# First K tiles ahead of the second group's transposes, R's first mixes two slots later, dummy matmuls between stages

## The chip, the cores and the metric

One Trainium2 chip, one core. The metric is device time in microseconds (us) of one execution. Several executions of the kernel before and of the other kernel are timed in turn on the same chip. Each set of runs is compared only with the runs of before that were taken beside it.

A ratio is the mean time of one kernel's fast runs over that of the other's of the same rounds, so not quite the ratio of the medians that are quoted. "Over before" in us is the difference of those two means.

## The reference

A causal depthwise convolution of seven taps with softmaxed weights per head, then an RWKV channel mix on its result:

```python
w = softmax(weight)                                   # 8 heads x 7 taps
y[b, t, h, :] = sum_k w[h, k] * x[b, t + k - 6, h, :]  # zeros ahead of t = 0
xk = mu_k * y + (1 - mu_k) * y_prev                    # y_prev: y one step earlier
xr = mu_r * y + (1 - mu_r) * y_prev
k = relu(xk @ w_k)            # 192 -> 1024
v = (k * k) @ w_v             # 1024 -> 192
out = sigmoid(xr @ w_r) * v   # x: 8 x 4160 x 192, float32
```

## The kernel before

Work goes in groups of 120-token blocks. For a group, PE convolves by Toeplitz matrices, ScalarE copies the result to `y`, and PE transposes it (early groups) into PSUM, from where VectorE (DVE) copies it to `yT`. From `yT` DVE takes the difference of neighbouring tokens and mixes it into `xk` and `xr`. Then, for each "slot", PE computes a K tile, ScalarE applies relu, DVE squares. R and V products follow some slots later. The program sets the order of each engine's instructions.

Everything that the change touches is in the prologue and in the first few slots:

```python
    psK = ctx.enter_context(tc.tile_pool(name="psK", bufs=2, ...))   # K tiles, dummies
    psM = ctx.enter_context(tc.tile_pool(name="psM", bufs=2, ...))   # conv, transposes, R
    four = ctx.enter_context(tc.tile_pool(name="four", bufs=4))      # relu results
    # ...
        warm = psK.tile([P, BANK], FP32, tag="k", name="warm")
        for _ in range(WARM):                       # WARM = 40
            nc.tensor.matmul(out=warm, lhsT=ones_t, rhs=zeros, start=True, stop=True)
        # ... softmax, Toeplitz matrix, loads of x, K weights, R weights, V weights
        for t in tails:
            nc.gpsimd.memset(t, 0.0)
        # ... convolution of group 0 and its copies
        for j in range(2):
            tr_mm(0, j)
        for j in range(2):
            tr_out(0, j, dve_)
        n = len(chunks(1))
        for c in range(n):
            conv_mm(1, c, ...)
            conv_out(1, c, act_)
        diff(0)
        for i in range(2):                          # i = 0: xk, i = 1: xr
            for part in range(2):
                mix(0, i, part)
        for j in range(2):                          # second group: transposes and copies
            tr_mm(1, j)
            tr_out(1, j, dve_)
        # ...
    # per pair of slots: K tiles, then by slot: act table, pe table, relu, dve table,
    # and the square of the slot before
```

## Time and profile before

| | before |
|---|---|
| timed ahead of the prediction, median of 3 | 467.15 us (466.83 to 467.34) |
| timed beside the changed kernel, median of 6 | 466.99 us (464.91 to 467.39) |
| the execution that the profile shows | 466.09 us, span 464.4 us |
| granted clock of PE over the span | 0.993, half from 14.5 to 21.4 us |

The difference between the time and the span is what lies outside the first and last instruction. Times in timelines count from the start of the span.

### The profile page before, as it was taken

The numbers are of one execution on the slowest core, as the hardware profiler recorded it, in microseconds if no ns is written. First come the engines' busy times: TensorE is split into PE (matmuls) and PEld (weight loads), VectorE is DVE, ScalarE is ACT, GpSimd is POOL, SyncE is SP. The second block draws the span as 40 slices with busy tenths as digits, with TensorE's granted clock in tenths as the row PEclk, the third lists the DMA queues.
The fourth block names the chain that finished last, engine by engine and source line by source line (L and its number), as shares of the span: only waits on it lengthen the run. The fifth ranks groups of instructions, "written<-read, shape, count | busy, mean of one in ns | idle before, by whom it ended". The sixth has DMA issues, their size and how long they took to land.

```text
span 464.4 us, 10001 instructions
## 1 busy us (share of the span) xinstructions
PE 445.4 (96%) x3898; PEld 298.3 (64%) x3960; DVE 387.3 (83%) x748; ACT 371.3 (80%) x544; POOL 49.5 (11%) x71
## 2 busy tenths in 40 slices
PE   8787999999999999999999999999999999999996
PEld 3554666666876666566676666666677666666676
DVE  2887799887998889889798989878898987888873
ACT  2598878978878897888979788887978888777771
POOL 6810511000020050000002041000002000000000
PEclk9799999999999999999999999999999999999999
DMA  5993999683469599755367779938166753821223
GB/s 79 164 185 75 181 196 202 120 192 112 105 136 186 141 154 232 148 145 135 99 150 124 182 120 215 220 82 200 55 150 129 165 133 95 167 69 52 69 69 95
DMA packets 134480, 64.18 MB, mean 138 GB/s; under 512 B 85825, under 2 KB 133985, under 8 KB 134433
## 3 DMA queue, kind: packets, MB, share of 16 engines
q1 hardware_dynamic: 96097, 48.60, 41.9%
q0 software_dynamic: 38336, 14.95, 27.7%
q8 instruction: 31, 0.51, 0.5%
q14 instruction: 16, 0.13, 0.1%
HBM read 29.65 MB, written 37.25 MB: 144 GB/s over the span
## 4 chain that ended last, share of the span: by engine, by line
PE 91%; DMA 2%; DVE 2%; ACT 2%; issue 2%; POOL 0%; DVEq 0%
PE ps_k L346 39%; PE ps_v L436 37%; PE ps_r L418 5%; PE ps_r L419 5%; PE ps_c L199 4%; DMA xb<-in_x_dram 1%; ACT k_sb L375 1%; PE ps_k L363 1%; DMA w_raw<-in_weight_dram 1%; ACT y L219 1%; PE ps_t L257 1%; DMA w_scr<-w_row 1%; DVE k L394 0%; ACT y L222 0%; DVE yT L268 0%
## 5 line engine op out<-in xcount | busy, mean ns | idle before, releaser
L375 ACT ACTIVATE k_sb<-ps_k 128x1024 bf16<-128x1024 f32 x260 | 260.1, 1026 | 36.4 <-PE ps_k L346 31.6
L346 PE MATMUL ps_k<-xk,wk 64*128 64x512 bf16 (+2 forms) x994 | 205.3, 377 | 7.5 <-ACT k_sb L375 0.4
L436 PE MATMUL ps_v<-wv,k 128*128 128x192 bf16 x2048 | 210.8, 246 | 0.0
L436 PEld LDWEIGHTS <-k 128*128 128x128 bf16 x2048 | 175.3, 98 | 31.3 <-issue 1.8
L394 DVE TENSOR_TENSOR k<-k_sb 128x1024 bf16<-128x1024 bf16 x256 | 174.9, 685 | 15.0 <-ACT k_sb L375 14.3
L346 PEld LDWEIGHTS <-wk 64*128 64x128 bf16 (+1 forms) x1056 | 56.3, 96 | 109.1 <-issue 108.0
L449 DVE TENSOR_TENSOR o_sb<-ps_v,r_sb 128x384 f32<-128x384 f32 x132 | 72.4, 549 | 35.7 <-PE ps_v L436 33.8
L426 ACT ACTIVATE r_sb<-ps_r 128x384 bf16<-128x384 f32 x132 | 64.4, 488 | 39.3 <-PE ps_r L419 38.8
L418 PE MATMUL ps_r<-wr,xr 128*128 128x192 bf16 x256 | 62.9, 246 | 0.0
L419 PE MATMUL ps_r<-wr,xr 128*128 128x192 bf16 x256 | 62.9, 246 | 0.0
L219 ACT CAST y<-ps_c 120x384 bf16<-120x384 f32 (+4 forms) x96 | 45.0, 471 | 8.8 <-PE ps_c L199 8.8
L199 PE MATMUL ps_c<-xb,toe 128*128 128x384 bf16 (+6 forms) x152 | 43.5, 321 | 4.1 <-ACT y L222 1.8
L323 DVE TENSOR_TENSOR xr<-xr,yT 128x1024 bf16<-128x1024 bf16 (+1 forms) x66 | 36.2, 549 | 2.3
L323 DVE TENSOR_TENSOR xk<-xk,yT 128x1024 bf16<-128x1024 bf16 (+1 forms) x66 | 36.2, 549 | 2.3
L109 POOL DMA_DIRECT2D xb<-in_x_dram x38 | 33.5, 888 | 31.0 <-issue 17.5
L281 DVE TENSOR_TENSOR d<-yT 128x1536 bf16<-128x1536 bf16 (+2 forms) x37 | 31.8, 859 | 3.6 <-DMA yT<-y_dram 3.5
L320 DVE TENSOR_SCALAR xr<-d,mu 128x1024 bf16<-128x1024 bf16 (+1 forms) x66 | 27.9, 423 | 0.1
L108 POOL DMA_DIRECT2D xb<-in_x_dram x8 | 4.4, 552 | 221.1 <-PE ps_k L346 221.1
L320 DVE TENSOR_SCALAR xk<-d,mu 128x1024 bf16<-128x1024 bf16 (+1 forms) x66 | 26.6, 403 | 0.2
L418 PEld LDWEIGHTS <-xr 128*128 128x128 bf16 x256 | 25.0, 98 | 0.0
L419 PEld LDWEIGHTS <-xr 128*128 128x128 bf16 x256 | 25.0, 98 | 0.0
L222 ACT CAST y<-ps_c 120x384 bf16<-120x384 f32 (+9 forms) x52 | 24.0, 466 | 0.4 <-DVE yT L227 0.2
(48 smaller groups left out, 88.5 us busy)
## 6 DMA issues: line engine op xcount, KB each, us to landing
out_dram<-o_sb SPq DMA_DIRECT2D x128, 192.0 KB, 2.4
xb<-in_x_dram POOLq DMA_DIRECT2D x18, 384.0 KB, 10.4
y_dram<-y SPq DMA_DIRECT2D x6, 720.0 KB, 5.4
y_dram<-y SPq DMA_DIRECT2D x4, 900.0 KB, 6.6
xb<-in_x_dram POOLq DMA_DIRECT2D x6, 432.0 KB, 8.1
y_dram<-y SPq DMA_DIRECT2D x3, 810.0 KB, 10.4
xb<-in_x_dram POOLq DMA_DIRECT2D x2, 480.0 KB, 8.8
xb<-in_x_dram POOLq DMA_DIRECT2D x4, 192.0 KB, 6.1
```

Source lines behind the costliest of these rows:

```text
L199: nc.tensor.matmul(out=ps[:, :, :, i * G : (i + 1) * G], lhsT=toe[:, h, :], rhs=xbs[g][:, :nb, :, h * G : (h + 1) * G], start=True, stop=True,
L219: copy(out=yh[:, :, :, c0 : c0 + n], in_=ps[:BLK, :, :, 0:n])
L320: nc.vector.tensor_scalar(out=o, in0=d[:, sl, :L], scalar1=mu[:, i, part : part + 1], scalar2=None, op0=ALU.mult)
L323: nc.vector.tensor_tensor(out=o, in0=o, in1=yT[:, sl, c0 : c0 + L], op=ALU.add)
L346: nc.tensor.matmul(out=ps[:, i, f * L : (f + 1) * L], lhsT=wk[r, 0 if hi else 1, fs], rhs=xk[r, i if hi else 2, :L], start=start and f == ...
L375: nc.scalar.activation(out=k_sb, in_=ps.rearrange("p a b -> p (a b)"), func=AF.Relu)
L394: nc.vector.tensor_tensor(out=o, in0=i, in1=i, op=ALU.mult)
L418: nc.tensor.matmul(out=o, lhsT=hi, rhs=wr[:, 0, :], start=True, stop=False)
L419: nc.tensor.matmul(out=o, lhsT=lo, rhs=wlo, start=False, stop=True)
L426: nc.scalar.activation(out=r_sb[:, :n, :], in_=ps[:, :n, :], func=AF.Sigmoid)
L436: nc.tensor.matmul(out=o, lhsT=k2[:, f, t * P : (t + 1) * P], rhs=wv[:, f, :], start=(f == 0), stop=(f == NF - 1),)
L449: nc.vector.tensor_tensor(out=o_sb[:, :n, :], in0=v_ps.pop(m)[:, :n, :], in1=r_sbs.pop(m)[:, :n, :], op=ALU.mult)
```

## The change

The intent: start ScalarE's stream of relus sooner by issuing the first two K tiles before the second group's transposes, take R's first mixes out of the way, and keep PE busy between stages so that its clock is not halved, as it is from 14.5 to 21.4 us in the profile of before. In the diff, `at(pe, n, ...)` puts a call into PE's table for slot n (`at(dve, ...)` into DVE's). Group 1 is the second group. A step is a stretch of tokens that is mixed together, and step 0 the first; `mix(s, 0, ...)` makes its `xk`, `mix(s, 1, ...)` its `xr`. The lines with `n0 == 4` move step 1's difference and mixes to other slots:

```diff
     for g, (p, blk0, nb, n0, on_pe) in enumerate(groups):
+        if g == 1:
+            for j in range((nb + 1) // 2):
+                at(pe, 0, tr_mm, g, j)
+                at(dve, 0, tr_out, g, j, nc.vector.tensor_copy)
         if g < 2:
             continue
@@
         if s == 0:
+            at(dve, 2, mix, s, 1, 0)
+            at(dve, 2, mix, s, 1, 1)
+            continue
+        if n0 == 4:
+            for n, fn, *a in ((0, diff), (0, mix, 0, 0), (1, mix, 0, 1), (3, mix, 1, 0), (4, mix, 1, 1)):
+                at(dve, n, fn, s, *a)
             continue
@@
+    def warm(n):
+        ps = psK.tile([P, BANK], FP32, tag="k", name="warm")
+        for _ in range(n):
+            nc.tensor.matmul(out=ps, lhsT=ones_t, rhs=zeros, start=True, stop=True)
@@
-        warm = psK.tile([P, BANK], FP32, tag="k", name="warm")
-        for _ in range(WARM):
-            nc.tensor.matmul(out=warm, lhsT=ones_t, rhs=zeros, start=True, stop=True)
+        warm(WARM)
@@
+        warm(2)
         for j in range(2):
             tr_mm(0, j)
         for j in range(2):
             tr_out(0, j, dve_)
+        warm(5)
@@
         diff(0)
-        for i in range(2):
-            for part in range(2):
-                mix(0, i, part)
-        for j in range(2):
-            tr_mm(1, j)
-            tr_out(1, j, dve_)
+        for part in range(2):
+            mix(0, 0, part)
+        warm(3)
```

## The prediction

> **What bounds the kernel now.** I read the page first. Over the whole span TensorE (PE) is the bound, and the chain that ended last is PE at 91%. The change touches only what is issued before slot 5, so the question is what sets the time of the first 45 us and whether a shift there reaches the end. The clock row of the page shows one slow slice near the start:
>
> ```profile
> PEclk9799999999999999999999999999999999999999
> ```
>
> So I cut the start into stretches (columns: stretch, its length, busy us and count of instructions of PE, weight loads, VectorE, ScalarE, GpSimd, then granted clock, DMA share, GB/s):
>
> ```profile
> 11.11:14.52 3.41, 1.80 (x20) 1.08 (x17) 1.46 (x5) 1.06 (x3) 3.07 (x5) 1.00 1.20 137
> 14.52:17.93 3.41, 2.64 (x19) 2.00 (x20) 3.09 (x10) 1.69 (x5) 1.95 (x4) 0.50 1.30 198
> 17.93:21.35 3.42, 3.42 (x23) 2.08 (x22) 3.25 (x6) 1.26 (x2) 3.42 (x6) 0.50 1.43 156
> 21.35:24.76 3.41, 2.87 (x24) 1.47 (x23) 3.34 (x7) 3.41 (x6) 1.71 (x2) 1.00 1.46 159
> 38.41:41.83 3.42, 1.89 (x16) 0.97 (x15) 3.02 (x7) 2.85 (x6) 0.00 (x0) 1.00 0.18 58
> ```
>
> The clock is halved from 14.52 to 21.35, after a stretch in which PE did little. But in 14.52 to 28 VectorE (DVE) is nearly always busy (3.09, 3.25, 3.34 of 3.41), so I read its own timeline:
>
> ```profile
> 16.25 0.35 DVE L320 TENSOR_SCALAR xr<-d,mu 128x512 bf16<-128x512 bf16 x1
> ...
> 17.29 0.29 DVE L323 TENSOR_TENSOR xr<-xr,yT 128x256 bf16<-128x256 bf16 x1
> 17.73 1.13 DVE L268 COPY yT<-ps_t 128x720 bf16<-128x720 bf16 x2
> 18.89 0.96 DVE L281 TENSOR_TENSOR d<-yT 128x1536 bf16<-128x1536 bf16 x1
> ...
> 27.03 0.53 DVE L268 COPY yT<-ps_t 128x720 bf16<-128x720 bf16 x1
> ```
>
> From 14.39, when the first difference starts, to 28.16 DVE idles for only some 0.2 us in all. The first R mixes of step 0 (16.25 to 17.58, four instructions, 1.33 us) lie exactly in the time in which PE transposes the second group; DVE would otherwise wait there. Last the chain itself in this region:
>
> ```profile
> 28.67 0.32 PE ps_t L257 x6
> 28.99 0.21 PE ps_c L199 x2
> 29.19 0.66 PE ps_v L436 x8
> 29.85 0.08 PE ps_r L418
> ```
>
> Line L199 at 28.99 is the first convolution of the fourth group. Its PSUM buffer is one of two that rotate under one tag, and by the order of allocations it is the buffer of the transposes that the copy at 27.03 to 27.56 empties. That wait has 28.99 - 27.56 = 1.43 us to spare now. From 31.1 to 44 the chain passes from engine to engine (ScalarE relus and casts, PE, DVE) with no DMA and no gap over 0.1 us, and from 44 on it is PE alone. I take a shift at 30 us to reach the end in full.
>
> [...] the stretch before the drop has 1.80 us of PE busy, 0.81 of it transposes; 38.41 to 41.83 has 1.89 and keeps the clock. [...] DVE sits idle 0.86 us before the copy at 29.02.
>
> **The change, part by part.**
> 1. Ten dummy matmuls (2, 5, 3) of 128x512. At full clock one costs 0.21 us (32 of them in 6.79 us). Two follow the first convolution at 12.10 and end at 12.53, before the transposes can start (12.59, waiting for ScalarE). Five follow the transposes at 13.69 and end at 14.77; the next convolution waits for its input until 14.85. Three follow that convolution. So none is on the path, and the stretch 11.11 to 14.52 gets about 0.43 + 0.83 = 1.26 us more of activity: 3.06 of 3.41. I expect full clock throughout. The second convolution then takes 8 x 0.08 = 0.65 us and not 1.44: 14.85 to 15.50, dummies to 16.15.
> 2. First K tiles. They need the xk mix (16.33) and the K weights. The weight loads are issued at 9.93, 10.46 and 10.99 and land 6.1, 6.2 and 6.3 us later: 16.1, 16.7, 17.3. The first tile's high half can go at 16.2, but its low half waits for the last load until 17.4. A tile costs 0.76 us at full clock (two took 1.52 in the chain at 121.13; two took 2.99 at half clock here). The low half's rest is about 0.25, so tile 0 ends at 17.65 and tile 1 at 18.4. Before, they ran from 18.08 to 21.07: ScalarE's first relu comes at 17.7 in place of 19.73, a lead of 2 us. That is the intended gain.
> 3. Second group's transposes. Now behind both tiles: start 18.4, six take 0.32, the copy starts 0.35 after the start (28.67 to 29.02 before). Copies 18.76 and 19.21, done 19.74. Before, they ran at 17.73 and were done at 18.86. So DVE gets them 0.88 us later, and it has nothing to do from 16.33 to 18.76: 2.4 us idle.
> 4. R's first mixes. They move from before the copies to after the first square. Same 1.33 us, but now behind the late copies. By the instruction order of the changed kernel DVE does: copies, difference 19.77, xk mixes 20.77 and 22.08, square 22.89, R mixes 23.49, square 24.81, then the same list as before from 22.61. That is 24.81 - 22.61 = 2.20 us late (0.88 + 1.32). The squares for slots 3 and 4 come at 27.87 and 28.47 and the copy at 29.07 to 29.60 (it waited 0.07 for PE before, which falls away).
>
> Sum at the convolution: 29.63 in place of 28.99, +0.64. Behind it the R product of the next tile pair waits for the second such copy (before 29.02 to 29.55, used at 29.85): DVE reaches it at 29.07 + 0.45 + 0.60 = 30.12, ends at 30.65, and the product goes at 30.68, +0.83 us. ScalarE has its lead no longer: it has four buffers for relu results, so relu 4 waits for the first square (23.57), relu 5 for the next (25.49), relu 6 for 27.22, relu 7 for 28.55, and then for the late convolution. Result: 467.15 + 0.83 = 468.0 us.
>
> **Rivals.**
> (a) Intended gain. If ScalarE's relus set the pace (3.41 busy of 3.41 in 21.35 to 24.76) and not DVE, the lead of 2.0 us would pass to the end: 465.1. For it: relu 0 is earlier, and the half clock costs PE some 3 us here. Against it: DVE is just as full before, all its work stays, and it gets 2.2 us of new idleness in front. I give it about one in six.
> (b) The clock drops all the same. With half clock the tiles end at 19.0, the copies come 1.2 us later than reckoned, and the chain is some 1.2 us worse: 469.2. Against it: 3.06 us of activity in the critical window, and 14.52 to 17.93 has dummies too. [...] One in eight.
> (c) It is absorbed. If the chain between 31 and 44 has slack that I do not see, or the weights land earlier and halve the DVE delay, the time stays at 467.2. About one in five.
>
> **Range and chances.** The mechanism gives +0.6 to +1.0 with the landings of this trace; these may move by half a microsecond, and executions before spread by 0.5 us. With the rivals the range is 466.3 to 469.2. The limits for 2% are 9.3 us away, over three times any shift here: faster 0.01, same 0.97, slower 0.02.
>
> **What would show it.** Granted clock 1.00 from 4.3 us on. First K matmul near 16.2 with a gap before the last low-half ones near 17.3. First relu near 17.7. DVE idle for 2 to 2.5 us before the copy near 18.8. The square of slot 0 near 22.9 (21.2 before) and of slot 1 near 24.8. Fourth group's first convolution near 29.6, released by the DVE copy, and steady PE work some 0.8 us later than before. It is wrong if that convolution starts by 29.0, if DVE's idle time before the copies is under 1 us, or if the time falls under 466.5.

## The result, and the profile after

| | before | changed |
|---|---|---|
| median of 6, same rounds | 466.99 us | 467.05 us (466.94 to 467.86) |
| ratio, 95% interval | | 1.0011 [0.9992, 1.0031] |
| difference of the means | | +0.52 us |
| profiled execution, span | 466.09, 464.4 us | 466.94, 465.2 us |

The time is the same within two per cent, as predicted, and inside the predicted range. Whether it is slower at all these six runs do not settle; a second set does (below: +1.11 us, interval clear of 1).

The stretches of the changed kernel at the times of those of before (in this execution the clock rose at 6.33 us, in that of before at 4.28; same columns: stretch, length, busy us of PE, weight loads, DVE, ScalarE, GpSimd, granted clock, DMA share, GB/s):

```profile
11.11:14.52 3.41, 3.06 (x26) 1.68 (x25) 0.54 (x2) 1.06 (x3) 3.10 (x5) 1.00 1.30 158
14.52:17.93 3.41, 3.41 (x32) 1.99 (x29) 2.62 (x7) 1.70 (x6) 1.93 (x4) 1.00 1.31 195
17.93:21.35 3.42, 3.11 (x39) 2.38 (x36) 2.28 (x4) 3.05 (x4) 3.42 (x6) 1.00 1.37 149
21.35:24.76 3.41, 2.59 (x16) 0.98 (x14) 3.27 (x10) 3.25 (x7) 1.87 (x3) 1.00 1.35 148
```

The clock stays at 1.00, and ScalarE has 3.05 us of work in the third stretch in place of 1.26: the relus do start early. DVE has 2.28 in place of 3.25. Its timeline shows where that went:

```profile
17.04 0.30 DVE L323 TENSOR_TENSOR xk<-xk,yT 128x256 bf16<-128x256 bf16 x1
19.00 0.97 DVE L268 COPY yT<-ps_t 128x720 bf16<-128x720 bf16 x2 [1.66 <-PE ps_t L257]
20.00 0.96 DVE L281 TENSOR_TENSOR d<-yT 128x1536 bf16<-128x1536 bf16 x1
...
23.46 0.35 DVE L320 TENSOR_SCALAR xr<-d,mu 128x512 bf16<-128x512 bf16 x1
...
24.50 0.29 DVE L323 TENSOR_TENSOR xr<-xr,yT 128x256 bf16<-128x256 bf16 x1
...
28.97 0.53 DVE L268 COPY yT<-ps_t 128x720 bf16<-128x720 bf16 x1
```

In brackets stand the idle time before an instruction and what ended it: 1.66 us waiting for the transposes, which now run behind the K tiles. The R mixes come at 23.46, behind the late copies, as the program orders them; the difference and `yT` that they read were there by 17.04, when the last `xk` mix read `yT`, and DVE idled all the same. The chain of waits then changes hands at the fourth group's first convolution:

```profile
27.85 1.20 DVE k L394 x2
29.05 0.45 DVE yT L268
29.51 0.04 issue
29.55 0.37 PE ps_c L199 x2
29.92 0.66 PE ps_v L436 x8
30.58 0.23 PE ps_r L418
```

Before, PE came to this convolution from its own work at 28.99. Now it waits for DVE's copy until 29.55, and the timeline of PE shows that it had nothing to do for 1.80 us:

```profile
27.27 0.48 PE L257 MATMUL ps_t<-ident,y 120*128 120x120 bf16 x6
29.55 0.37 PE L199 MATMUL ps_c<-xb,toe 128*128 128x240 bf16 x2 [1.80 <-DVE yT L268]
```

So the lead of the first K tiles was built up and then spent waiting. DVE's first output product comes at 31.79 (30.92 before), +0.87 us, and the span is 0.8 us longer. From there on both kernels do the same work.

### The profile page after: what moved, and what is told of

It reads as the page before. It is cut to its first block, busy times and chain, and to the rows that moved or that the text cites. A ratio compares the mean times of both kernels' runs of the same rounds, so it can differ in the third digit from the quotient of the medians.

```text
span 465.2 us, 10084 instructions
## 1 busy us (share of the span) xinstructions
PE 453.3 (97%) x3970; PEld 298.0 (64%) x3970; DVE 386.7 (83%) x748; ACT 371.7 (80%) x544; POOL 49.4 (11%) x71
## 4 chain that ended last, share of the span: by engine, by line
PE 95%; DVE 3%; ACT 1%; issue 0%; DVEq 0%
PE ps_k L346 40%; PE ps_v L436 37%; PE ps_r L418 5%; PE ps_c L199 5%; PE ps_r L419 5%; PE warm L528 3%; DVE k L394 1%; PE ps_k L363 1%; DVE yT L268 1%; DVE xr L323 0%; ACT k_sb L375 0%; DVE xr L320 0%; PE ps_t L257 0%; ACT y L219 0%; ACT y L222 0%; DVE xk L323 0%
## 5 line engine op out<-in xcount | busy, mean ns | idle before, releaser
L346 PE MATMUL ps_k<-xk,wk 64*128 64x512 bf16 (+2 forms) x1056 | 214.6, 375 | 0.7 <-DVE xk L323 0.5
```

The source lines that it names most:

```text
L346: nc.tensor.matmul(out=ps[:, i, f * L : (f + 1) * L], lhsT=wk[r, 0 if hi else 1, fs], rhs=xk[r, i if hi else 2, :L], start=start and f == ...
```

## The experiments

Nine kernels were built, all correct; the changed kernel, the kernel before and one of the nine were run once more. Two numbers read from each profile tell most of the story. "Copies" is the start of the second group's copies on DVE, "conv 4" the start of the fourth group's first convolution on PE, both in us from the span's start.

| kernel | ratio to before, 95% | over before, us | copies | conv 4 | between |
|---|---|---|---|---|---|
| before (first profile / one look) | | | 17.73 / 18.03 | 28.82 / 29.16 | 11.09 / 11.13 |
| changed, first set | 1.0011 [0.9992, 1.0031] | +0.52 | 19.00 | 29.55 | 10.55 |
| changed, again | 1.0026 [1.0007, 1.0044] | +1.11 | 19.21 | 29.87 | 10.66 |
| dummies only | 0.9990 [0.9978, 1.0003] | -0.44 | 19.96 | 29.32 | 9.36 |
| dummies, early K | 0.9996 [0.9984, 1.0008] | -0.19 | 19.56 | 29.19 | 9.63 |
| early K, late R (no dummies) | 1.0042 [1.0018, 1.0066] | +1.63 | 18.67 | 29.34 | 10.67 |
| the same, one look | | | 20.68 | 31.36 | 10.68 |
| late R only | 1.0001 [0.9988, 1.0014] | +0.07 | 18.14 | 29.70 | 11.56 |
| R mixes twice, late | 1.0059 [1.0041, 1.0077] | +2.74 | 19.25 | 31.16 | 11.91 |
| R mixes twice, once in the idle time | 1.0035 [1.0018, 1.0052] | +1.65 | 19.87 | 30.50 | 10.63 |
| dummies, tails on DVE | 0.9978 [0.9964, 0.9991] | -1.05 | 19.20 | 28.99 | 9.79 |
| the same, 34 dummies at the start | 0.9968 [0.9954, 0.9982] | -1.52 | 17.61 | 27.32 | 9.71 |
| the same, with early K | 0.9993 [0.9977, 1.0008] | -0.35 | 19.00 | 29.00 | 10.00 |

How to read it: in the kernels whose profiles show conv 4 waiting for DVE (that is all but before, late R only, and the one at 27.32, where PE arrives from its own work), "between" is the length of DVE's list. It is 9.4 to 10.0 us without the R mixes in it, 10.6 to 10.7 with them, 11.9 with them twice. When the list starts is set by PE, by the transposes, except where a long R mix (1.75, 1.44 and 0.70 us in three profiles, below) keeps DVE busy. For the kernel before, 28.82 and 29.16 are the starts in the timeline; in both PE works on its transposes for another 0.16 to 0.17 us, so that the first profile's chain puts the convolution at 28.99.

That a shift of conv 4 reaches the end in full can be read off the same profiles: in eleven of the fourteen, the execution's time is conv 4 plus 437.25 to 437.49 us. The three others are the two doubled kernels (439.02 late, 438.89 idle), whose clock is halved for some 3.4 us after conv 4, and the kernel at 27.32 (437.89), which loses some 0.5 us of its lead later on.

The theory: in the changed kernel DVE sets the pace from the copies to conv 4, so late copies and R mixes behind them both cost, and the early K tiles win nothing. Rivals: the early relus are what helps; only the clock counts; the R mixes are hidden. Four kernels of one chip first take the change apart.

### Dummies only

```diff
 # the changed kernel with the order of before restored:
-        if g == 1: ...            # transposes of group 1 in slot 0
-            at(dve, 2, mix, s, 1, 0)
-            at(dve, 2, mix, s, 1, 1)
-        if n0 == 4: ...           # step 1 on its own slots
         warm(3)
+        for part in range(2):
+            mix(0, 1, part)
+        for j in range(2):
+            tr_mm(1, j)
+            tr_out(1, j, dve_)
```

> Only the ten dummy matmuls are kept; the order of the kernel before is restored (R mixes, then the second group's transposes, then the K tiles). Theory (VectorE sets the pace from the second group's copies to the fourth group's first convolution): its list is as before, only the copies come at 17.66 at once after the R mixes, so the fourth group's first convolution is no longer held by PE at half clock (1.43 us of spare before) and comes near 27.5 to 28.3; time 0.7 to 1.4 us under before. Rival (the early K tiles are what helps): no gain without them, within 0.3 us of before. Rival (only the clock counts): the clock is 1.00 from about 4 to 6 us on, and the time is 1 to 2 us under before whatever VectorE does.

Measured: 466.14 us median of 5, 0.44 us under before, an interval that includes 1. So this run alone decides nothing between the theory and the first rival; that the mean clock was 0.999 in the profile and the gain of 1 to 2 us did not come speaks against the second. Conv 4 came at 29.32 where 27.5 to 28.3 was expected. The profile tells why in its execution: the copies came at 19.96, not 17.66. About 1.5 us of this is one R mix, 0.28 us elsewhere, that took 1.75 us; most of the rest is a first stage that ended later (first convolution at 12.42, 11.44 in before). These are DVE's line and, below it, GpSimd's:

```profile
17.96 1.75 DVE L320 TENSOR_SCALAR xr<-d,mu 128x256 bf16<-128x256 bf16 x1
```

```profile
17.69 0.93 POOL L154 DMA_DIRECT2D wv<-in_moe_w_v_dram  x1 [0.29 <-DMA wk<-in_moe_w_k_dram]
18.62 1.01 POOL L558 MEMSET tail<- 128x512 bf16 x2
```

The mix began inside GpSimd's issue of the V weights, and ended at 19.71, 0.08 us after the second of GpSimd's memsets (19.63), though GpSimd went on to the next loads of `x` at once. This was not foreseen; it gets its own experiment below.

### Dummies and early K tiles, R mixes in their old place

```diff
-            at(dve, 2, mix, s, 1, 0)
-            at(dve, 2, mix, s, 1, 1)
@@
         warm(3)
+        for part in range(2):
+            mix(0, 1, part)
```

> Dummies and early K tiles are kept, the R mixes go back to their old place ahead of the copies, where VectorE sat idle in the changed kernel. Theory: VectorE idles 0.3 to 0.5 us in place of 1.7 before the copies (still near 18.8 to 19.0), and all behind them comes 1.2 to 1.33 us earlier than in the changed kernel: fourth group's first convolution near 28.3, time about 1.2 us under the changed kernel and 0.5 to 0.9 us under before. Rival (the late R mixes cost nothing because they are hidden): the same time as the changed kernel.

Measured: 466.59 us, 0.19 us under before, so some 0.7 us (0.52 + 0.19) to 1.3 us (1.11 + 0.19) under the changed kernel's two sets. DVE's list is 9.63 us long and not 10.55: about 0.9 of the 1.33 us of mixes come out of it. The hidden-mixes rival expected the time of the changed kernel. The difference in time is of other rounds and too small to refute it alone; DVE's shorter list speaks against it, and the doubled kernels below decide. Conv 4 came at 29.19, not 28.3. The idle time did not shrink as expected: it is still 2.02 us, because in this execution the input and the K weights landed late, and the first pair of K tiles could go on with its low halves only at 18.05, which put the copies at 19.56. So the early K order is also exposed to the landing of the weights.

### Early K tiles and late R mixes, no dummies

```diff
-        warm(2)
@@
-        warm(5)
@@
-        warm(3)
```

> The changed kernel without its ten dummies. Theory: the clock is halved from some 14.5 to 16.5 us on for one or two windows of 3.4 us, the two K tiles take 3 us in place of 1.55, the copies come near 20.0 and the time is 0.8 to 1.5 us over the changed kernel. Rival (the dummies are off the path and the early K tiles alone keep the clock): clock 1.00 all along and the time of the changed kernel.

Measured: 467.81 us median, 466.73 to 471.14, 1.63 us over before. The profiled execution was the fastest and kept full clock (mean 1.000), which fits the rival; the others spread upwards. A single further look, of state unknown as there is one run only, was taken to see what a slow one is:

> The changed kernel without its ten dummies, one more look. Its timed runs spread from 466.7 to 471.1 and the one profiled was the fastest, at full clock. Theory: in the slow ones the clock is halved for one or two windows, so a run over 467.3 shows half clock somewhere between 14 and 28 and a fourth group's first convolution after 30.0; a run at 466.7 to 467.2 shows none. If a run over 468 shows full clock throughout, the spread has another cause.

It took 468.76 us. Its stretches (columns as above) and its two pairs of K tiles on PE:

```profile
14.00:18.00 4.00, 2.37 (x22) 1.50 (x20) 2.64 (x7) 1.96 (x6) 1.78 (x4) 0.86 1.29 199
18.00:20.00 2.00, 2.00 (x13) 1.10 (x13) 0.00 (x0) 1.02 (x1) 1.84 (x4) 0.50 1.33 154
```

```profile
17.05 3.18 PE L346 MATMUL ps_k<-xk,wk 128*128 128x256 bf16 x16 [0.70 <-DVE xk L323]
...
21.43 1.69 PE L346 MATMUL ps_k<-xk,wk 128*128 128x256 bf16 x16
```

Half clock from 16.90 to 20.31, the first pair in 3.18 us and the second, at full clock, in 1.69; copies at 20.68 and conv 4 at 31.36, 2.0 us behind the profiled fast one (29.34), and the time 2.03 us behind it (466.73). Not all of that is the half clock's: the first K tile starts at 17.05 here and at 16.20 in the fast one, because the clock first rose at 6.66 and not at 4.86 us. (These two are estimates from the end of the 40 dummies, 12.77 and 11.88 us: in the profile of before a dummy takes 0.43 us ahead of the clock's rise at 4.28 and 0.21 behind it.) The slower pair accounts for the other 1.2 us.

The clocks of the timed runs say more. With one half-clock stretch of 3.4 us the mean clock is 0.996 (this look from 16.90 to 20.31, and the doubled kernels' profiles); the profiles without such a stretch show 0.998 to 1.000. Without the dummies one of six runs shows 1.000, the one of 466.73 us, four show 0.996 and the one of 471.14 us shows 0.989. Of the changed kernel's eleven runs, nine show 0.998 to 1.000 and two 0.996. So the dummies do work: they keep the half clock away in most executions, though not in all. What the slowest run had in addition was not looked at.

### Late R mixes only

```diff
 # before, with only this (and step 1 on the changed kernel's slots):
-        for i in range(2):
-            for part in range(2):
-                mix(0, i, part)
+        for part in range(2):
+            mix(0, 0, part)
@@
+            at(dve, 2, mix, s, 1, 0)      # s == 0
+            at(dve, 2, mix, s, 1, 1)
```

> Only the R mixes are moved (no dummies, transposes ahead of the K tiles as before). Theory: VectorE idles 1.3 to 1.4 us until the copies at 17.7 and then carries 1.33 us more ahead of the fourth group's first convolution, which uses up the 1.43 us of spare: that convolution near 29.0, time within 0.3 us of before. Rival (the late mixes cost their full length): 1.3 us over before.

Measured: 466.95 us, +0.07 us. DVE idled 0.91 us ahead of the copies. The spare time that before has at conv 4 took the late mixes: conv 4 starts at 29.70, right behind PE's own transposes, and DVE's copy had ended at 29.19 (28.66 + 0.53), 0.5 us ahead. The late mixes alone cost nothing; they cost when the copies are late too.

### The changed kernel and before once more, and the R mixes twice

These four ran together on a second chip. The doubled kernels do the same four R mixes a second time into the same tile, which changes no result:

```diff
 # R mixes twice, late
             at(dve, 2, mix, s, 1, 1)
+            at(dve, 2, mix, s, 1, 0, True)    # True: no new tile
+            at(dve, 2, mix, s, 1, 1, True)
 # R mixes twice, once in the idle time
+        for part in range(2):                 # ahead of warm(3)
+            mix(0, 1, part)
@@
-            at(dve, 2, mix, s, 1, 0)
-            at(dve, 2, mix, s, 1, 1)
+            at(dve, 2, mix, s, 1, 0, True)
+            at(dve, 2, mix, s, 1, 1, True)
```

> The changed kernel once more, on the chip of the runs beside it. Theory: the profiled execution of the kernel before was a fast one (466.09 against 466.83 to 467.34 timed), so the 0.83 us of the prediction belong on 466.1 and the changed kernel stands near 466.9 to 467.2, 0.2 to 0.7 us over the mean of before. If instead the cost is 0.83 us over the mean of before: 467.6 to 467.8.

Measured: 467.49 us, ratio 1.0026 [1.0007, 1.0044], +1.11 us. This set shows the changed kernel slower by a little, and by more than the 0.2 to 0.7 us that the theory expected here. The first set gave +0.52; 0.83 lies between and in both intervals. The two sets differ in their clocks: two of these five runs, 468.36 and 468.39 us, are the two with 0.996. The three others, at 0.998 to 1.000, took 467.04 to 467.49 us, on average 0.66 us over before. These two were not profiled, so where their clock fell is not known.

> The kernel before once more, one look. [...] Theory: the half clock lasts one or two windows again somewhere between 14 and 24, the copies of the second group come at 17.5 to 18.5, the fourth group's first convolution at 28.9 to 30.0, in step with the time of the execution. If the first convolution stays at 29.0 while the time differs by over 0.5 us, the spread comes from elsewhere.

Measured: 466.41 us (one look), half clock for 6.83 us again, 15.57 to 22.40, copies at 18.03 and conv 4 at 29.16. As expected, though 0.3 us of difference in time is too little to say more.

> The changed kernel with the four late R mixes done a second time into the same tile, at the same late place (behind the first square). Theory (VectorE sets the pace there): their 1.0 to 1.33 us come in full, fourth group's first convolution near 30.7, time 1.0 to 1.3 us over the changed kernel. Rival (hidden beside PE and ScalarE): the changed kernel's time within 0.3 us.

Measured: 469.25 us, +2.74 us over before, 1.64 over the changed kernel beside it, more than the 1.0 to 1.3 expected. Conv 4 at 31.16, 1.29 us later than there.

> The changed kernel with the R mixes done once in VectorE's idle time ahead of the copies and once more at the late place: the same work as in the other doubled kernel. Theory: the idle time of 1.7 to 2.0 us takes the first doing for nothing, so the time is that of the changed kernel within 0.3 us and 1.0 to 1.3 us under the other. Rival (total VectorE work counts, not its place): the same time as the other doubled kernel.

Measured: 468.07 us, +1.65 us over before: 1.09 us less than the other doubled kernel for the same work, and 0.55 us over the changed kernel where under 0.3 was expected. The first copies and the copy ahead of conv 4, late doubling and idle doubling:

```profile
19.25 0.97 DVE L268 COPY yT<-ps_t 128x720 bf16<-128x720 bf16 x2 [2.44 <-PE ps_t L257]
...
30.58 0.53 DVE L268 COPY yT<-ps_t 128x720 bf16<-128x720 bf16 x1
```

```profile
18.18 1.44 DVE L320 TENSOR_SCALAR xr<-d,mu 128x256 bf16<-128x256 bf16 x1
...
19.87 0.97 DVE L268 COPY yT<-ps_t 128x720 bf16<-128x720 bf16 x2
...
29.92 0.52 DVE L268 COPY yT<-ps_t 128x720 bf16<-128x720 bf16 x1
```

DVE's list is 1.25 us longer (11.91 against 10.66) with the second doing in it, and as long as in the changed kernel (10.63) with it in the idle time. That is the mechanism by itself: DVE sets the pace, and the same work costs its full length behind the copies and does not lengthen the list ahead of them. It was not free there: the long mix came again (1.44 us in place of 0.28, ended 0.08 us after the memsets did) and delayed the copies to 19.87, and conv 4 by 0.63 us against the changed kernel's second profile. Both profiled executions also show half clock for some 3.4 us (from 32.55 and from 30.61, mean clock 0.996), after a stretch in which PE waited for DVE (busy for 1.61 and 1.58 of the 3.41 us ahead); this adds about 1.5 us to each behind conv 4 (439.02 and 438.89 from there to the end, where the others have 437.25 to 437.49). Setting aside the runs with such a stretch, by their mean clock (0.996 or less), leaves two of the late doubling (468.45 and 468.57 us), four of the idle one (467.53 to 468.38) and three of the changed kernel. The late doubling then costs 1.24 us, which is the 1.25 us of the list, and the idle one 0.56.

### The tail memsets moved to DVE's idle time, and fewer dummies at the start

```diff
 # on top of "dummies only"
-        for t in tails:
-            nc.gpsimd.memset(t, 0.0)
@@
         softmax()
+        for t in tails:
+            nc.vector.memset(t, 0.0)
```

> The dummies-only kernel with the two tail memsets moved from GpSimd to VectorE's idle time near 5.5 to 6. In the dummies-only profile one R mix of VectorE (128x256, elsewhere 0.28 us) took 1.75 us, and ended 0.1 us after GpSimd's tail memsets did. If the memsets hold that mix up: it takes 0.28 to 0.4 us here, the copies come near 18.3 to 18.5 in place of 19.96, and the time is up to 1.4 us under the dummies-only kernel in executions where the two met. If something else held it up: as the dummies-only kernel, 466.1, with such long mixes again in some executions.

Measured: 465.85 us, 1.05 us under before, interval [0.9964, 0.9991]. The expected 0.28 to 0.4 us and copies at 18.3 to 18.5 were missed: the mix took 0.70 us and the copies came at 19.20. The long mix, and GpSimd beside it:

```profile
18.25 0.70 DVE L320 TENSOR_SCALAR xr<-d,mu 128x256 bf16<-128x256 bf16 x1
```

```profile
18.00 0.93 POOL L154 DMA_DIRECT2D wv<-in_moe_w_v_dram  x1
```

It now ends at 18.95, 0.02 us after the issue of the V weights (18.93). In all three profiles in which this R mix was long it began inside that issue; it ended 0.08 us after the memsets where these followed, and 0.02 us after the issue where they did not. What lengthens the mix three profiles do not show. The gain over "dummies only" is 0.6 us in the means (1.05 - 0.44); the sets are on the same chip but not of the same rounds, and their intervals overlap.

```diff
-    WARM = 40
+    WARM = 34
```

> As the run beside it, and with 34 dummies in place of 40 at the start. In profiles where the clock rises late (near 6.3 us) the 40 end near 12.4, 1.3 us after the Toeplitz matrix has landed (10.9); 34 end near 11.1. Theory: the first convolution comes at 11.1 to 11.4 in either case, the R mixes end by 17.5, and the time is 0 to 0.8 us under the run beside it. Rival (input landings at 14.7 to 15.5 and the K weights at 17.3 to 18.0 hide it): no difference over 0.3 us.

Measured: 465.21 us, 464.92 to 465.63, ratio 0.9968 [0.9954, 0.9982], 1.52 us under before. It beats both kernels. The first convolution comes at 10.87 (12.71 in the run beside it), the R mixes are done before GpSimd's issue at 17.83, and the copies wait for PE only:

```profile
16.79 0.29 DVE L323 TENSOR_TENSOR xr<-xr,yT 128x256 bf16<-128x256 bf16 x1
17.61 0.97 DVE L268 COPY yT<-ps_t 128x720 bf16<-128x720 bf16 x2 [0.53 <-PE ps_t L257]
...
26.51 0.53 DVE L268 COPY yT<-ps_t 128x720 bf16<-128x720 bf16 x1
```

Part of that 10.87 is the clock's rise, which fell at 4.06 us here and at 6.87 in the other (estimates as above, from the end of the dummies at 10.20 and 12.88 us). In this profile DVE no longer sets the pace: from 15 to 37 us the chain has no DVE instruction in it.

How much of the 1.52 us is the clock alone was not separated. The kernel before hints at it: of its 42 timed runs beside the experiments, three show a mean clock of 0.998 or 0.999, and took 465.07, 465.12 and 466.54 us; the 39 with less took 465.89 to 467.73. So twice the kernel before, at a mean clock of 0.998 or 0.999, was as fast as the best kernel.

### Early K tiles on the best kernel

```diff
 # the best kernel, with only the two K tiles ahead of the second group's transposes
+        if g == 1:
+            for j in range((nb + 1) // 2):
+                at(pe, 0, tr_mm, g, j)
+                at(dve, 0, tr_out, g, j, nc.vector.tensor_copy)
@@
-        for j in range(2):
-            tr_mm(1, j)
-            tr_out(1, j, dve_)
 # (and step 1 on the changed kernel's slots)
```

> The best kernel so far (dummies, R mixes in their old place, tail memsets on VectorE, 34 dummies at the start; 0.9968 of before) with the one part of the change that it lacks: the two K tiles ahead of the second group's transposes. Theory: the transposes then wait for the K weights (17.3 or later) and two tiles, the copies come at 18.7 to 19.5 in place of 17.6, VectorE idles some 2 us ahead of them, and the time is 0.6 to 1.3 us over the best kernel: 0.998 to 0.9996 of before. Rival (the early relus pay once VectorE is not overloaded): at or under 0.9968.

Measured: 466.36 us, ratio 0.9993, so 1.17 us more over its before than the best kernel over its own (-0.35 against -1.52; another chip). The copies come at 19.00 after 1.69 us of idle time:

```profile
19.00 0.97 DVE L268 COPY yT<-ps_t 128x720 bf16<-128x720 bf16 x2 [1.69 <-PE ps_t L257]
```

With the R mixes in their old place, the tail memsets off GpSimd and a mean clock of 1.000 in the profile, the early K tiles (with the slots of step 1 that go with them) still make the kernel slower. Conv 4 comes 1.68 us later than in the best kernel, the copies 1.39; an `xk` mix at 21.00 that took 0.97 us, 0.55 in the best kernel, adds to the rest. The rival that the early relus pay is out.

## Why the prediction was right

**The increment.** Predicted +0.83 us; measured +0.52 and +1.11 us in the two sets, and +0.85 and +0.86 between the profiled executions of before and changed in the two sets. Neither set of times alone is fine enough to test 0.83; the steps behind it are, because they are points of time in the profile. The mechanism held: late copies, R mixes behind them, conv 4 waiting for DVE, no lead left for ScalarE. That the figure fits so closely is in part luck, as parts 1 to 3 show.

**The absolute time was the weak term.** 468.0 was predicted and 467.05 and 467.49 measured, inside the range of 466.3 to 469.2 but 0.5 to 0.95 us under the figure. The 0.83 us came from a profile of an execution at 466.09 us and were added to the median of 467.15. On the profiled execution they would give 466.92, and the changed kernel's profiled execution took 466.94. This suggests that points of time from a profile belong on that execution's time. The second set, whose expectation was built on it, did not confirm it for the median (467.49 where 466.9 to 467.2 was expected).

**Part 1, dummies.** Full clock throughout: right in the profile (1.00 in all four stretches above). Two things were wrong. The clock was assumed to rise at 4.3 us; it rose at 6.33 here, so the first 40 dummies ended 1 us later (12.61 against 11.60 in before) and the second convolution ran at 15.62, not 14.85. By then its input had landed, so the five dummies and the three are on the path, where none was expected:

```profile
14.70 1.08 PE warm L528 x5
15.78 0.66 PE ps_c L199 x8
16.44 0.65 PE warm L528 x3
17.09 1.55 PE ps_k L346 x16
```

What they cost is small. From the start of the first convolution to that of the second it is 3.17 us here, and 2.95 and 2.92 in the two without dummies; to the first K tile it is 4.51 against 4.48 and 4.44.

**Part 2, K tiles.** Expected from 16.2 with a gap until the last weights, and a first relu at 17.7. They ran from 16.96 without the gap, and the first relu came at 17.92. Two errors met here: the late start and the wait for the weights that it made needless, and the second hid most of the first. That is luck. In the four other profiles with early K tiles in which the clock rose before 5.3 us (estimates, as above), the gap did show (a low half at 17.16, 17.49, 17.74 and 18.05); in the three others, with a rise after 6.4, it did not.

**Parts 3 and 4, copies and mixes.** Copies at 18.76 predicted, 19.00 measured; idle time 2.4 us predicted, 1.66 measured, since the xk mix ended at 17.34 and not 16.33. Squares at 22.89 and 24.81 predicted, 22.86 and 24.71 measured. Conv 4 at 29.63 predicted, 29.55 measured; the R product at 30.68 and 30.58. The doubled kernels confirm the step by itself.

**Rivals.** (a) the intended gain fails: from relu 4 on ScalarE waited for DVE's squares, as the prediction said (relu 4 at 23.64 us against 25.03 before, relu 7 at 30.41 against 29.69), and the early K tiles cost on the best kernel too. (b) the half clock did not come in the changed kernel's two profiles, and may have come in the two of its runs with 0.996; without its dummies five of six timed runs show 0.996 or less. (c) absorption fails: extra DVE work at that place shows in full in conv 4 (1.25 us more of it, conv 4 1.29 us later).

## What to carry to other kernels

When several engines are nearly full, starting one of them earlier is worth nothing if the order that does it starves another (here the early K tiles left DVE idle for 1.69 us on the best kernel and cost 1.17): look at which engine's list is unbroken up to the next hand-over, and fill that engine's idle time first. Work that stands in front of a wait can be free; the same work behind it costs its length once the spare time there is used up (the late R mixes alone: +0.07 us; their second doing behind the copies: 1.24). Look at the mean clock of each timed run before comparing means: here one half-clock stretch of 3.4 us went with about 1.5 us in the doubled kernels, and the change cost 0.52 and 1.11. For effects of a microsecond, check the other executions' times before adding a difference read from one profile, and look for single instructions that take several times their usual length beside another engine's work (here 1.75 us in place of 0.28).

## What these runs leave open

- The long R mix. A 128x256 tensor_scalar of VectorE, elsewhere 0.28 us, took 1.75, 1.44 and 0.70 us, each time from within GpSimd's issue of one weight load (0.93 us) to 0.02 us after its end or, in the first two, 0.08 us after that of the two memsets that followed it (1.01 us together). Beside other DMA issues of GpSimd such an operation was sometimes not longer (128x512, 0.35 us at 17.24 in the first of these profiles; 128x1024, 0.49 us at 21.00 in the changed kernel) and sometimes it was (128x1024, 0.98 us at 21.20 with the tails on DVE; one of 0.97 us is in the last kernel, whose GpSimd was not looked at). Beside which issues VectorE takes longer, and why, these runs do not settle.
- The drops of the clock. In six profiles PE was busy for 1.58 to 1.80 of the 3.41 us ahead of a drop, while after other stretches of that length with 1.89, 1.92 and once 1.61 us the clock stayed full. PE's busy time in the profile does not tell the two apart.
- The first rise of the clock. It fell between 4.06 and 6.87 us in these profiles (4.28 and 6.33 in the traces of before and changed, the others estimates as above), and the 40 dummies ended between 11.55 and 12.88 us (first convolution at 11.38 to 12.71). What that is worth in time was not separated.
